# Attention steps dealt by a written table, and weights' splits issued ahead of them, in a fused attention, MoE and GLU kernel

## The chip, the core and the metric

The kernel runs on one core of one Trainium2 chip. The metric is the device time of one launch in microseconds (us): the median of three runs of the kernel before is 1403.98 us (1403.47 to 1404.71).

## What is computed

Three layers follow each other, all in float32. B = 2, H = 8 heads, S = 768, D = 64; N = B·S = 1536 tokens of width 512.

```python
# 1: attention, banded (96 local positions) plus 8 global keys, with a distance bias
scores = scale * q @ k.T + bias
a = softmax(where(is_global | is_local, scores, -1e9))
x = (a @ v) laid out as tokens x 512
# 2: MoE with 8 experts, gate P balanced by 8 Sinkhorn rounds
out = sum_e P[:, e:e+1] * (relu(x @ w1[e]) @ w2[e])        # w1[e]: 512 x 1024
# 3: gated linear unit
y = (sigmoid(out @ w_gate) * (out @ w_val)) @ w_out        # 512 x 1536 and back
```

## The kernel before

A product of float32 matrices is made of three TensorE passes over operands that are split into a high and a low part: `product` (lines 360 to 362) issues high·high, high·low and low·high. ScalarE (ACT) writes a high part by a copy that rounds, and GpSimd (POOL) or VectorE (DVE) subtracts it from the source for the low part: `split_one`, lines 203 and 204. The weights of an expert come in quarters; a quarter of `w1` and of `w2` lies in a buffer `raw` (two of them) and is split in halves, each half one ACT and one POOL instruction of 128x512.

The MoE is a row of **visits**, each one quarter of an expert for some tokens. A visit has two first products (12 passes of 128x384, ACT writes the relu `hh`, DVE the rest `hl`, lines 410 and 411), and after the first product of the next visit come its three second products (6 passes of 128x512). After each product `run_visit` calls `tick`. A tick does two things: `side`, a step of work that belongs elsewhere, and `ahead`, which splits the weights that come next (`ahead_steps`: the two halves of the next visit's `w1`, the two halves of this visit's `w2`, then `load`, two DMAs of 512 KB each that fill the `raw` buffer just freed). All DMAs of this stage are issued on SyncE's queue (SP), in program order.

In the first five visits (`NA` = 5) the side work is the second half of the attention: `banded_steps` yields a first part, then `None`, then 20 **attention steps** (`both`, here called s0 to s19). Each step issues the scores of two blocks of 128 queries (PE, line 981), their weights (DVE line 992, then two ACT exponentials each, line 998), the transposes of earlier weights (PE line 1023, copied out by ACT, line 1024: `aT`), the value products of still earlier ones (PE line 1037), and in half of the steps the transposes of the next q and k (PE line 924, copied out by ACT, line 930: `qT`, and by DVE: `kT`) with their loads. Transposes and products share a ring of four PSUM banks, so a product waits until the bank's last reader is done.

Ahead of the visits, two products of visit 0 are **begun** (`begun`: 9 of 12 passes); visit 0 ends them with 3 passes each. During the first part of the attention a pacer called `weights` splits the first weights. `Paced` deals a list of steps evenly over a number of ticks: with 20 steps over 18 ticks, each tick has one step, but the ninth and the last have two. The ticks are two in visit 0 (it has no second products ahead of it) and five in each later visit.

Of the kernel before, what the change touches and what calls it, by code (L numbers as in the profile page):

```python
# [33 lines left out]
class Ring:  # L34
    def __init__(self, items):
        self.items = list(items)
        self.n = 0
# [6 lines left out]
class Paced:  # L44
# [8 lines left out]
    def tick(self):  # L53
        self.n += 1
        upto = min(len(self.steps), len(self.steps) * self.n // self.ticks)
        while self.done < upto:
            self.steps[self.done]()
            self.done += 1

    def finish(self):  # L60
        while self.done < len(self.steps):
            self.steps[self.done]()
            self.done += 1


@with_exitstack
def tile_global_local_attention__then__sinkhorn_moe__then__glu(
# [100 lines left out]
    NA = NQ + 1  # L168
# [37 lines left out]
    def split_halves(r, h, lo, eng=nc.gpsimd):  # L206
        for half in range(2):
            cols = slice(half * 2 * FQ, (half + 1) * 2 * FQ)
            yield lambda cols=cols: split_one(r[:, cols], h[:, cols], lo[:, cols], eng)
# [5 lines left out]
    def second_steps(n):  # L215

        vis = visits[n]
        if vis["kind"] == "gate":
            return
        if vis["kind"] == "val":  # L220
            r = piece(vis["piece"] + 1)
        else:
            r = raw[vis["raw"]][:, 4 * FQ : 8 * FQ]
        eng = nc.vector if n == G0 + 1 else nc.gpsimd
        yield from split_halves(r, wh[vis["slot"]][1], wl[vis["slot"]][1], eng)

    def first_steps(n):

        vis = visits[n]
        if vis["load"]:  # L230
            r = raw[vis["raw"]][:, 0 : 4 * FQ]
            yield from split_halves(r, wh[vis["slot"]][0], wl[vis["slot"]][0])

    def ahead_steps(n):


        if 0 < n < F0 - 1:
            yield from first_steps(n + 1)
        if visits[n]["load"]:
            yield from second_steps(n)  # L240
            yield lambda b=visits[n]["raw"]: load(b)
# [16 lines left out]
    def sum_steps(n):  # L258

        a, (s1, s2, s3, s4) = w1_blocks(n), sums()  # L260
        for out, x, y, op in (
            (s1, a[1, 0], a[1, 1], ALU.add), (s2, s1, a[0, 0], ALU.subtract),
            (s4, a[0, 1], s2, ALU.subtract), (s3, a[0, 0], a[1, 0], ALU.subtract),
        ):
            yield lambda out=out, x=x, y=y, op=op: nc.gpsimd.tensor_tensor(
                out=out, in0=x, in1=y, op=op
            )

    def form_step(n, i):
        a, (s1, s2, s3, s4) = w1_blocks(n), sums()  # L270
        src = (a[0, 0], s1, s2, s4, s3, a[0, 1], a[1, 1])[i]
        h, lo = form(i)
        split_one(src, tall(h), tall(lo))
# [123 lines left out]
    def unit_first(n, c, tick):  # L397
        vis = visits[n]
        m = c[1] * P
        at = next_hid()  # L400
        hh, hl = hid[at]
        for f in range(2):
            w = wh[vis["slot"]][0], wl[vis["slot"]][0]
            if state["begun"]:
                ps = state["begun"].pop(0)
                first(w, c, f, ps, range(KD - 1, KD))
            else:
                ps = state["A"].next()[:, :m]
                first(w, c, f, ps)
            nc.scalar.activation(out=hh[:, f, :m], in_=ps, func=AF.Relu)  # L410
            nc.vector.scalar_tensor_tensor(
                out=hl[:, f, :m], in0=ps, scalar=0.0, in1=hh[:, f, :m].bitcast(F32),
                op0=ALU.max, op1=ALU.subtract,
            )
            tick()
        return [(n, c[0] + j, at, j) for j in range(c[1])]
# [30 lines left out]
    def flush(tick):  # L447
        pending, state["pending"] = state["pending"], []
        for unit in pending:
            unit_second(*unit)  # L450
            tick()

    def run_visit(n, tick, ahead, pace=None):


        chunks = visits[n]["chunks"]
        ahead = Paced(ahead, (chunks[0][1] + 2) * len(chunks) * (pace or PACE) // 12)
        side = tick

        def tick():  # L460
            side()
            ahead.tick()

        for c in chunks:
            pending = unit_first(n, c, tick)
            flush(tick)
            state["pending"] = pending
        ahead.finish()
# [237 lines left out]
    with tc.tile_pool(name="attn", bufs=1) as ap:  # L706
# [187 lines left out]
        def banded_tiles(fp):  # L894
            t = {}
            t["qT"] = [fp.tile([P, C], F32, name=f"qT{i}") for i in range(2)]
            t["kT"] = [fp.tile([P, UB, KW], F32, name=f"kT{i}") for i in range(2)]
            t["ks"] = [fp.tile([P, NG + NW], F32, name=f"ks{i}") for i in range(NP)]
            t["e"] = Ring(fp.tile([P, 2, KW], F32, name=f"e{i}") for i in range(LAG + 2))
            t["mn"] = Ring(fp.tile([P, 2], F32, name=f"mn{i}") for i in range(LAG + 2))  # L900
            sums = fp.tile([P, LAG + 2, 2, 2], F32, name="sums")
            nc.gpsimd.memset(sums, EPS)
            t["rs"] = Ring(sums[:, i] for i in range(LAG + 2))
            t["rr"] = Ring(fp.tile([P, 2], F32, name=f"rr{i}") for i in range(2))
            t["aT"] = Ring(fp.tile([P, 2, 2, P], F32, name=f"aT{i}") for i in range(2))
            return t
# [225 lines left out]
        with tc.If(banded > 0) as cmp:  # L1132
            with tc.tile_pool(name="banded", bufs=1) as fp:
                t = banded_tiles(fp)
                shared = Ring([bank[2], bank[3], bank[6]])
                state.update(S=bank[0:2], O=Ring(bank[4:6]), T=shared, X=shared)
                steps = list(banded_steps(t))
                begin = steps.index(None)
                weights = Paced([*[no_tick] * 5, *first_steps(0), no_tick], begin)

                def widen():
                    ring = state["T"]
                    at = ring.n % 3
                    ring = Ring([bank[7], *ring.items[at:], *ring.items[:at]])
                    state.update(T=ring, X=ring, A=ring, Y=ring)

                state["widen"] = widen
                for n, step in enumerate(steps[:begin]):
                    step()
                    weights.tick()  # L1150
                side = Paced(steps[begin + 1 :], 5 * NA - 7)
                early = list(first_steps(1))
                early.pop(0)()
                for n in range(NA):
                    run_visit(n, side.tick, [*early, *ahead_steps(n)])
                    early = []
                side.finish()
# [263 lines left out]
    side = Paced(gate_steps(), 5 * (NB0 - NA) + 5 * CB * NQ - 4)  # L1421
# [8 lines left out]
    for n in range(NA, F0):  # L1430
# [6 lines left out]
        if n < F0 - 1:  # L1437
# [3 lines left out]
        ahead = [  # L1441
            *ahead_steps(n), *sum_steps(F0), *(lambda i=i: form_step(F0, i) for i in range(4)),
            *second_steps(F0),
        ]
# [66 lines left out]
```

## Time and profile before

| | |
|---|---|
| Median of 3 runs | 1403.98 us |
| The profiled execution's own time | 1403.86 us |
| Its span, first to last instruction | 1402.1 us |
| TensorE busy | 1387.4 us, 99% |
| VectorE, ScalarE, GpSimd busy | 918.0, 564.8, 644.5 us |
| TensorE idle in 40 to 50 us, 50 to 60, 130 to 140 | 1.61, 0.70, 0.74 us |
| TensorE idle in 300 to 800 us | 0.0 us |

The profile is one execution. PE's matmuls are pipelined, so the distance between the starts of two of them says more than their durations. "PEld" is the loading of weights into the array. An idle time in brackets is that of the engine just before the row, with the instruction that ended it.

### The profile page before, as it was taken

How to read it: one execution, taken by the hardware profiler on the slowest of the kernel's cores; microseconds unless marked ns; L12 is line 12 of the kernel's file. 1: busy time of each engine (PE TensorE's matmuls, PEld its weight loads, DVE VectorE, ACT ScalarE, POOL GpSimd, SP SyncE). 2: the span in 40 equal slices, each digit the busy share in tenths (PEclk: the TensorE clock that was granted, in tenths of full speed). 3: DMA queues.
4: the chain of work that ended last, by engine and by line, in shares of the span. 5: the costliest groups of instructions: out<-in, count | busy, mean ns of one | idle time of the engine just before them, and what ended most of it. 6: DMA issues, size and time to landing. Idle time of an engine off the chain costs nothing. (4 is left out here: it accounts for less than half of the span.)

```text
span 1402.1 us, 20701 instructions
## 1 busy us (share of the span) xinstructions
PE 1387.4 (99%) x7425; PEld 1237.5 (88%) x7425; DVE 918.0 (65%) x1776; ACT 564.8 (40%) x1334; POOL 644.5 (46%) x757
## 2 busy tenths in 40 slices
PE   8999999999999999999999999999999999999998
PEld 5777799999999999999999999999999899999997
DVE  7676486776667667666776666667675665555446
ACT  6776323333333333333333333333333464444441
POOL 5664335534454453444545444454453464443440
PEclk9999999999999999999999999999999999999999
DMA  7860101212121222212212222121212011010002
GB/s 180 183 163 21 48 29 46 84 67 75 53 76 53 75 74 85 76 55 74 76 53 82 77 76 75 54 75 54 75 53 68 16 31 46 16 46 31 31 1 91
DMA packets 98944, 92.67 MB, mean 66 GB/s; under 512 B 55056, under 2 KB 73488, under 8 KB 98832
## 3 DMA queue, kind: packets, MB, share of 16 engines
q1 hardware_dynamic: 98544, 91.26, 21.3%
q8 instruction: 60, 0.98, 0.3%
q14 instruction: 52, 0.43, 0.1%
q10 hardware_dynamic: 288, 0.00, 0.0%
HBM read 78.66 MB, written 12.58 MB: 65 GB/s over the span
## 5 line engine op out<-in xcount | busy, mean ns | idle before, releaser
L435 DVE SCALAR_TENSOR_TENSOR acc<-bank,gate,acc 128x512 f32<-128x512 f32 x336 | 251.4, 748 | 229.1 <-PE bank L362 224.3
L204 POOL TENSOR_TENSOR wl<-raw,wh 128x256 fp32r<-128x256 f32 (+1 forms) x218 | 222.9, 1038 | 346.7 <-ACT wh L203 333.2
L360 PE MATMUL bank<-wh,hh 128*128 128x512 f32 x912 | 359.0, 394 | 0.4 <-DVE work L655 0.2
L362 PE MATMUL bank<-wh,hl 128*128 128x512 f32 x912 | 357.3, 392 | 0.0
L361 PE MATMUL bank<-wl,hh 128*128 128x512 f32 x912 | 355.9, 390 | 0.0
L360 PE MATMUL bank<-xh,wh 128*128 128x384 f32 x768 | 259.5, 338 | 1.7 <-DVE kept L551 0.9
L362 PE MATMUL bank<-xh,wl 128*128 128x384 f32 x768 | 257.6, 335 | 0.9 <-POOL wl L204 0.6
L361 PE MATMUL bank<-xl,wh 128*128 128x384 f32 x768 | 257.9, 336 | 0.0
L541 ACT ACTIVATE hh<-kept 128x384 fp32r<-128x384 f32 x168 | 88.2, 525 | 308.1 <-DVE kept L551 308.1
L362 PEld LDWEIGHTS bank<-wh,hl 128*128 128x128 f32 x912 | 171.1, 188 | 37.9
L204 POOL TENSOR_TENSOR wl<-work,wh 128x256 fp32r<-128x256 f32 x160 | 126.7, 796 | 148.3 <-ACT wh L203 147.9
L360 PEld LDWEIGHTS bank<-wh,hh 128*128 128x128 f32 x912 | 171.3, 188 | 24.2 <-DVE acc L435 0.8
L361 PEld LDWEIGHTS bank<-wl,hh 128*128 128x128 f32 x912 | 171.4, 188 | 22.7
L555 ACT ACTIVATE kept<-bank 128x384 f32<-128x384 f32 x240 | 117.4, 490 | 173.3 <-PE bank L362 171.9
L360 PE MATMUL bank<-th,wh 128*128 128x384 f32 x480 | 161.4, 336 | 0.0
L362 PE MATMUL bank<-th,wl 128*128 128x384 f32 x480 | 161.3, 336 | 0.0
L361 PE MATMUL bank<-tl,wh 128*128 128x384 f32 x480 | 161.0, 335 | 0.0
L551 DVE TENSOR_TENSOR kept<-bank,kept 128x384 f32<-128x384 f32 x240 | 132.2, 551 | 35.4 <-PE bank L362 34.8
L360 PEld LDWEIGHTS bank<-xh,wh 128*128 128x128 f32 x768 | 144.1, 188 | 12.6 <-ACT qT L930 1.5
L361 PEld LDWEIGHTS bank<-xl,wh 128*128 128x128 f32 x768 | 144.3, 188 | 9.3
L362 PEld LDWEIGHTS bank<-xh,wl 128*128 128x128 f32 x768 | 144.3, 188 | 1.0 <-POOL wl L204 1.0
L543 DVE SCALAR_TENSOR_TENSOR hl<-kept,hh 128x384 fp32r<-128x384 f32 x168 | 116.4, 693 | 1.4 <-ACT hh L541 1.4
(149 smaller groups left out, 1691.9 us busy)
## 6 DMA issues: line engine op xcount, KB each, us to landing
raw<-in_moe_w_dram SPq DMA_DIRECT2D x72, 512.0 KB, 4.3
glw<-work SPq DMA_DIRECT2D x36, 256.0 KB, 2.4
raw<-glw SPq DMA_DIRECT2D x18, 512.0 KB, 3.9
work<-in_moe_w_gate_dram SPq DMA_DIRECT2D x12, 512.0 KB, 3.9
work<-in_moe_w_val_dram SPq DMA_DIRECT2D x12, 512.0 KB, 4.3
work<-in_moe_w_out_dram SPq DMA_DIRECT2D x12, 512.0 KB, 3.8
qr<-in_q_dram SPq DMA_DIRECT2D x32, 96.0 KB, 3.0
kr<-in_k_dram SPq DMA_DIRECT2D x32, 96.0 KB, 2.8
```

Of the source, the lines that this page charges most:

```text
L204: eng.tensor_tensor(out=lo, in0=r, in1=h.bitcast(F32), op=ALU.subtract)
L360: nc.tensor.matmul(lhsT=ah, rhs=bh, start=first, stop=False, **mm)
L361: nc.tensor.matmul(lhsT=ah, rhs=bl, start=False, stop=False, **mm)
L362: nc.tensor.matmul(lhsT=al, rhs=bh, start=False, stop=end, **mm)
L435: nc.vector.scalar_tensor_tensor(out=a, in0=ps, scalar=gate[:, t, e : e + 1], in1=a, op0=ALU.mult, op1=ALU.add,)
L541: nc.scalar.activation(out=hh, in_=src, func=AF.Relu)
L543: lambda: nc.vector.scalar_tensor_tensor(out=hl, in0=src, scalar=0.0, in1=hh.bitcast(F32), op0=ALU.max, op1=ALU.subtract,)
L551: nc.vector.tensor_tensor(out=p, in0=ps, in1=kept, op=ALU.add)
L555: nc.scalar.activation(out=snap[:, i], in_=ps, func=AF.Copy)
```

## The change

Three edits, all in the attention stage: the 20 steps are dealt by a written list of counts (none at the first tick, which lies between the two begun products, two at the second tick of visits 2 and 3, one at each of the others up to the second tick of visit 4); in the first five visits a tick runs `ahead` before `side`; and the first weights' two splits are placed at 7/10 and 8/10 of the first part, not at 6/8 and 7/8.

```diff
+class Planned(Paced):
+
+    def __init__(self, steps, counts):
+        super().__init__(steps, len(counts))
+        self.counts = counts
+
+    def tick(self):
+        if self.n < len(self.counts):
+            for step in self.steps[self.done : self.done + self.counts[self.n]]:
+                step()
+            self.done += self.counts[self.n]
+        self.n += 1
...
         def tick():
-            side()
-            ahead.tick()
+            if n < NA:
+                ahead.tick()
+                side()
+            else:
+                side()
+                ahead.tick()
...
-                weights = Paced([*[no_tick] * 5, *first_steps(0), no_tick], begin)
+                weights = Paced([*[no_tick] * 6, *first_steps(0), *[no_tick] * 2], begin)
...
-                side = Paced(steps[begin + 1 :], 5 * NA - 7)
+                side = steps[begin + 1 :]
+                counts = [0, 1, *[1] * 5, *[1, 2, 1, 1, 1] * 2, 1, 1]
+                assert sum(counts) == len(side)
+                side = Planned(side, counts)
```

The first place is TensorE at the end of the two begun products (banks 70 and 65; `wh_80` and `wl_84` are visit 0's weights, `kT` and `qT` those of step s0). Before:

```order
L362 MATMUL bank_70<-xh,wl_84 128x384
L981 MATMUL bank_63<-kT_242,qT_240 128x256
L981 MATMUL bank_64<-kT_242,qT_240 128x256
L981 MATMUL bank_63<-kT_243,qT_241 128x256
L981 MATMUL bank_64<-kT_243,qT_241 128x256
L924 MATMUL bank_66<-ident,qr_120 128x128 x3
L924 MATMUL bank_69<-ident,kr_124 128x128 x3
L1023 MATMUL bank_70<-ident,e_250 128x128 x4
L360 MATMUL bank_65<-xh,wh_80 128x384
```

With the change:

```order
L376 MATMUL bank_70<-xh,wl_84 128x384
L374 MATMUL bank_65<-xh,wh_80 128x384
L375 MATMUL bank_65<-xl,wh_80 128x384
L376 MATMUL bank_65<-xh,wl_84 128x384
L999 MATMUL bank_63<-kT_242,qT_240 128x256
L999 MATMUL bank_64<-kT_242,qT_240 128x256
L999 MATMUL bank_63<-kT_243,qT_241 128x256
L999 MATMUL bank_64<-kT_243,qT_241 128x256
L942 MATMUL bank_66<-ident,qr_120 128x128 x3
L942 MATMUL bank_69<-ident,kr_124 128x128 x3
L1041 MATMUL bank_70<-ident,e_250 128x128 x4
L374 MATMUL bank_65<-xh,wh_82 128x384
```

The end of the second begun product now stands ahead of s0, and a whole product of visit 1 (`wh_82`) stands between s0 and s1.

The second place is ScalarE from the first product of visit 1 on. `wh_81` is visit 0's `w2`, `wh_83` visit 1's, and the `wh_80` here is visit 2's `w1`, split out of `raw_88` after that buffer's second load. Before:

```order
L203 ACTIVATE wh_81<-raw_88 128x512 x2
L410 ACTIVATE hh_78<-bank_69 128x384
L998 ACTIVATE e_251,sums<-e_251,mn_256 128x256 x2
L930 ACTIVATE qT_241<-bank_70,qs 128x384
L998 ACTIVATE e_252,sums<-e_252,mn_257 128x256 x2
L1050 ACTIVATE xh<-bank_67 128x384
L1024 ACTIVATE aT_263<-bank_66 128x512
L1024 ACTIVATE aT_262<-bank_69 128x512
L203 ACTIVATE wh_80<-raw_88 128x512
```

With the change:

```order
L217 ACTIVATE wh_81<-raw_88 128x512
L424 ACTIVATE hh_78<-bank_65 128x384
L217 ACTIVATE wh_80<-raw_88 128x512
L1016 ACTIVATE e_249,sums<-e_249,mn_254 128x256 x2
L1016 ACTIVATE e_250,sums<-e_250,mn_255 128x256 x2
L1042 ACTIVATE aT_263<-bank_66 128x512
L1042 ACTIVATE aT_262<-bank_69 128x512
L424 ACTIVATE hh_78<-bank_70 128x384
L217 ACTIVATE wh_80<-raw_88 128x512
L217 ACTIVATE wh_83<-raw_89 128x512
L1016 ACTIVATE e_251,sums<-e_251,mn_256 128x256 x2
L948 ACTIVATE qT_241<-bank_65,qs 128x384
```

Visit 2's first split of `w1` stood behind step s2 (exponentials of `e_251` and `e_252`); it now stands ahead of step s1 (`e_249` and `e_250`). On SP every row up to and past the load that fills `raw_88` for it stands as before.

The third place is GpSimd in the first part (`wl_84`: the low half of visit 0's first weights; `e`: POOL's share of the attention's normalisation). Before:

```order
L1011 TENSOR_SCALAR e_252<-e_252,rr_261 128x128
L1011 TENSOR_SCALAR e_248<-e_248,rr_260 128x256
L204 TENSOR_TENSOR wl_84<-raw_88,wh_80 128x512
L1011 TENSOR_SCALAR e_249<-e_249,rr_261 128x256
L204 TENSOR_TENSOR wl_84<-raw_88,wh_80 128x512
```

With the change:

```order
L1029 TENSOR_SCALAR e_252<-e_252,rr_261 128x128
L218 TENSOR_TENSOR wl_84<-raw_88,wh_80 128x512
L1029 TENSOR_SCALAR e_248<-e_248,rr_260 128x256
L218 TENSOR_TENSOR wl_84<-raw_88,wh_80 128x512
L1029 TENSOR_SCALAR e_249<-e_249,rr_261 128x256
```

Both subtractions moved up by one place, past the normalisations of `e_248` and `e_249`.

## Rows read from the trace of the kernel before

**Rows 1.** The page: TensorE's busy time, and its granted clock in 40 slices

```profile
PE 1387.4 (99%) x7425; PEld 1237.5 (88%) x7425; DVE 918.0 (65%) x1776; ACT 564.8 (40%) x1334; POOL 644.5 (46%) x757
...
PEclk9999999999999999999999999999999999999999
```

**Rows 2.** Busy times by stretch: stretch, sum, PE, PEld, DVE, ACT, POOL, PEclk, DMA, GB/s

```profile
300.00:800.00 500.00, 500.00 (x2516) 452.41 (x2515) 342.06 (x555) 178.06 (x396) 234.52 (x256) 1.00 0.21 71
```

**Rows 3.** Timeline, PE, 45 to 59 us: start us, us, engine line op out<-in xcount [idle before]

```profile
45.14 1.47 PE L981 MATMUL bank<-kT,qT 64*128 64x256 f32 x8 [0.56 <-DVE mn L992]
...
48.33 1.06 PE L1023 MATMUL bank<-ident,e 128*128 128x128 f32 x8 [0.92 <-DVE hl L411]
...
...
51.41 1.13 PE L981 MATMUL bank<-kT,qT 64*128 64x256 f32 x8
52.47 1.09 PE L1037 MATMUL bank<-aT,vo 128*64 128x128 f32 x16
...
55.95 0.45 PE L360 MATMUL bank<-xh,wh 128*128 128x384 f32 x1 [0.70 <-ACT qT L930]
...
58.23 1.14 PE L981 MATMUL bank<-kT,qT 64*128 64x256 f32 x8
```

**Rows 4.** Timeline, SP, 52 to 56 us: the issues around the second load of raw

```profile
52.45 0.96 SPq L724 DMA_DIRECT2D kr<-in_k_dram  x2
53.52 1.96 SPq L187 DMA_DIRECT2D raw<-in_moe_w_dram  x2
```

**Rows 5.** Line 187's DMA of 53.52 us, issue to landing; then all eight to 75 us

```profile
DMA to landing us min/median/max: 4.4/4.4/4.4
...
DMA to landing us min/median/max: 4.1/4.8/5.3
```

**Rows 6.** Timeline, ACT, 58 to 65 us

```profile
58.47 0.63 ACT L203 ACTIVATE wh<-raw 128x512 fp32r<-128x512 f32 x1
58.99 0.49 ACT L410 ACTIVATE hh<-bank 128x384 fp32r<-128x384 f32 x1
60.45 0.51 ACT L998 ACTIVATE e<-e,mn 128x256 f32<-128x256 f32 x1 [0.96 <-DVE mn L992]
...
61.45 0.56 ACT L930 ACTIVATE qT<-bank,qs 128x384 f32<-128x384 f32 x1
...
63.25 1.06 ACT L1024 ACTIVATE aT<-bank 128x512 f32<-128x512 f32 x2
64.21 0.62 ACT L203 ACTIVATE wh<-raw 128x512 fp32r<-128x512 f32 x1
```

**Rows 7.** Timeline, 134 to 136 us: the last attention step's copy and its value products

```profile
134.72 0.60 ACT L1024 ACTIVATE aT<-bank 128x512 f32<-128x512 f32 x1 [1.17 <-PE bank L1023]
135.37 0.42 PEld L1037 LDWEIGHTS bank<-aT,vo 128*64 128x64 f32 x8 [0.97 <-ACT aT L1024]
135.37 0.66 PE L1037 MATMUL bank<-aT,vo 128*64 128x128 f32 x8 [0.74 <-ACT aT L1024]
```

**Rows 8.** PEld at the start (512-column filler), then clock and busy times after the last matmul

```profile
1.58 0.15 PEld L763 LDWEIGHTS <-zeros 128*128 128x128 bf16 x1 [0.28 <-issue]
...
4.57 0.15 PEld L763 LDWEIGHTS <-zeros 128*128 128x128 bf16 x1 [0.28 <-issue]
4.99 0.31 PEld L763 LDWEIGHTS <-zeros 128*128 128x128 bf16 x2 [0.27 <-issue]
...
1401.00:1402.10 1.10, 0.00 (x0) 0.00 (x0) 0.00 (x0) 0.00 (x0) 0.00 (x0) 0.51 0.00 0
```

**Rows 9.** Timeline, PE, 87 to 90 us: the two steps of the ninth tick

```profile
87.77 1.26 PE L981 MATMUL bank<-kT,qT 64*128 64x256 f32 x8 [0.44 <-DVE mn L992]
...
89.54 1.21 PE L1037 MATMUL bank<-aT,vo 128*64 128x128 f32 x12 [0.51 <-ACT aT L1024]
```

**Rows 10.** Timeline, POOL, 33 to 38 us: a normalisation and the second low half

```profile
33.71 0.96 POOL L1011 TENSOR_SCALAR e<-e,rr 128x256 f32<-128x256 f32 x1
36.68 1.28 POOL L204 TENSOR_TENSOR wl<-raw,wh 128x512 fp32r<-128x512 f32 x1 [2.01 <-ACT wh L203]
```

## The prediction

> **What bounds the kernel now.** I read the page first: TensorE (PE) is busy 99% of the span, and its granted clock is full in every slice [rows 1]. So the kernel gets shorter only where PE stands still, and a new standstill counts in full: there is no slack behind it, since PE has no idle time at all from 300 to 800 us [rows 2]. Then I went through PE's timeline in the stretch that the change touches. There the waits are short: 0.56 us for VectorE ahead of the scores of step s1, 0.92 us ahead of its transposes, 0.70 us ahead of the second product of visit 1 [rows 3]; 0.44 and 0.51 us in the ninth tick, whose two steps have no product between them [rows 9]; 0.74 us at the end, where the last step follows the one before it directly [rows 7]. Together 3.87 us: this is about all that better dealing can win. Last I read SP and ACT, because the change moves ACT's splits, and a split waits for a DMA.
>
> **The split that moves ahead of its data.** Visit 2's first weights come from the second load of buffer raw 0. Its issue on SP starts at 53.52 us, right behind the issues before it (52.45 and 0.96 us) [rows 4], and lands 4.4 us later, at 57.92 [rows 5]. ACT takes it at 58.47 [rows 6]: only 0.55 us to spare. Nothing on SP ahead of this load is moved, and SP was not waiting but issuing, one DMA in about 0.5 us, so I take 57.92 for the changed kernel too.
>
> In the order of the changed ACT this split stands two attention steps and a product sooner: behind the relu of visit 1's first product, ahead of the exponentials of s1. That product had ended by 51.41 us before [rows 3], and now has one attention step less ahead of it, so ACT is there before 51 us and stands until 57.92. Behind it in ACT's queue are the four exponentials of s1 and the two copies `aT`; the value products of s2 wait for these on PE. PE reaches them early: before at 52.47 us, now with the second product of visit 1 also done (55.95 to 58.23, 2.28 us) and with the waits of 0.56 and 0.92 us gone, by some 53.3 us [rows 3].
>
> ACT from 57.92, each duration from the distance of starts [rows 6]: the split 0.52 (58.47 to 58.99), two pairs of exponentials 1.0 each (60.45 to 61.45), so the copies begin at 60.44. PE follows 0.65 us after such a copy begins (134.72 to 135.37) [rows 7]: it resumes at **61.1 us**, after standing for nearly 8. ACT goes on: the second copy ends at 60.44 + 0.96 = 61.40 (63.25 to 64.21 for two), the relu of visit 1's second product 0.5, two splits 1.04, a pair of exponentials 1.0, `qT` 0.56: 64.5. The next product, the first second product of visit 1, takes the PSUM bank that `qT` empties, so it starts at about 64.6. PE meanwhile needs 2.8 us for the rest of s2 (52.47 to 55.95, less the wait of 0.70), to 63.9, and waits once more.
>
> At this point the changed PE has done both begun products, s0 to s2 and both first products of visit 1. Before, the same set was done at 58.23 [rows 3]. The loss is 64.6 - 58.23 = **6.4 us**. The gains in between (2.18 us of waits) are inside it: because the end is pinned to a landing, coming sooner only lengthens the wait.
>
> **The clock after the wait.** Nothing in the trace before has PE idle for 8 us between matmuls. At the two ends of the run it shows this: after the last matmul the granted clock is still full for some 3 us and then falls (0.51 as the mean of the last 1.1 us), and when PE starts from rest, the filler of 512 columns loads its weights every 0.42 to 0.43 us from 1.58 to 4.99 us [rows 8], which is the lower level, 1.2 GHz, though the clock column says 1.00 there. I therefore take the clock to fall in the wait, and price the new start by these rows, 3.5 us at the lower level. From 61.1 these do half of 3.5 = 1.75 us of the 2.8, the rest goes at full speed: 65.7 in place of 64.6, **+1.1 us**, since part lies beside ACT's queue. Ends: 0 (the clock holds), 1.9 (half of 3.8, nothing covered). The Trainium skill, TensorE: Matmul & The Clock Gate, section on what matters for your kernels, says that an idle gap between bursts of matmuls puts PE back to half rate and asks to avoid such gaps: by that rule the sum stands, without it the time is 1.1 us lower; no run here has yet shown it inside a program.
>
> **The dealing.** The list puts two steps on the second tick of visit 3 where one stood, and takes the pair at the end apart. The nearest row for a pair without a product between is the ninth tick: 0.44 + 0.51 = **+0.95 us** [rows 9]; ends 0 and 1.9, as its exponentials are all full-width. The pair at the end had a wait of 0.74 us [rows 7], now covered by a whole product: **-0.74 us**; ends 0 and -0.97, PEld's figure.
>
> **The first splits.** They gain nothing in this sum, for whatever begins sooner ends in the wait of 57.92. By themselves they would be near zero as well: on POOL the second low half (1.28 us) now stands ahead of the normalisation of `e_249` (33.71 us) [rows 10], and waits for its ACT half; so PE would wait for that normalisation where it waited for the low half.
>
> **Sum.** 6.4 + 1.1 + 0.95 - 0.74 = 7.7 us on the profiled execution's 1403.86: **1411.6 us**; the median of the runs, 1403.98, lies 0.1 above that execution, which changes nothing here.
>
> **Rivals.** *The data is there in time* (not slower): if the load landed before ACT arrives, the change would do what its list says: -2.18 - 0.74 + 0.95 = -2.0, so 1401.9. The place is the second load of raw 0, the price one us for each us of landing, and it decides at about 57.92 - 7.7 = 50.2 us: an issue at some 45.8, about 15 issues of SP sooner. For it speaks that the split waited for nothing before, and that SP's time of issue comes from one execution; against it that SP issues without a gap and nothing of it is moved up. 5% for this, 3% for half of it. *The clock holds*: the same wait, 1410.5; for it, that no row shows a fall between matmuls. 25%. *More is late behind the wait*: the loads of q for step s8 wait for PE to read that buffer in s2, so SP stands too, and with it the loads of v and the next raw, each some 8 us later; against it, these had ten us and more to spare. One more wait of 3 us gives 1414.6. 10%. The forecast keeps 57%.
>
> **How the numbers follow.** Landing times of this load's kind lie between 4.1 and 5.3 us [rows 5], so -0.3 to +0.9; with the clock at 0 and the second pair at 0 the forecast's own range begins at 1409.2, and with all high ends it reaches 1415. I give 1407.5 to 1414.5: it takes in the clock's rival, most of the later waits and some of a shorter wait, and leaves out the first rival. A measurement of this kernel tells about 0.2% (2.8 us) from no change: faster 0.04, same 0.05, slower 0.91.
>
> **What would show it.** Right: ACT idle some 8 us ahead of a split (line 217) until a raw DMA, near 49 to 58 us; PE's value products (line 1055) waiting for `aT` to about 61; the rows of 0.56, 0.92 and 0.70 us gone; a granted clock under 1 after the wait; a pair of waits in the second tick of visit 3. Wrong: that split without a wait, or a landing well before 55 us; then the reading of SP as bound by its issues has failed.

## The result, and the profile after

The changed kernel takes 1411.48 us (median of 5 runs, 1410.96 to 1412.37) against 1403.98 before: ratio 1.0054, interval [1.0043, 1.0066]. The forecast was 1411.6, in a range from 1407.5 to 1414.5. The profiled execution took 1411.96 us with a span of 1410.1, where the span before was 1402.1: 8.0 us more in the spans, 7.5 in the medians. Times below are medians without one execution, of the kernel with four issues sooner, that took 1522.8 us at a granted clock of 0.851.

The page of the changed kernel, TensorE's (PE's) busy time and granted clock, answers to [rows 1]; one slice is no longer full:

```profile
PE 1389.7 (99%) x7425; PEld 1240.1 (88%) x7425; DVE 917.4 (65%) x1776; ACT 564.8 (40%) x1334; POOL 644.2 (46%) x757
...
PEclk9899999999999999999999999999999999999999
```

PE's timeline where the two begun products end, which answers to [rows 3]:

```profile
52.10 1.14 PE L999 MATMUL bank<-kT,qT 64*128 64x256 f32 x8
61.21 1.97 PE L1055 MATMUL bank<-aT,vo 128*64 128x128 f32 x16 [7.98 <-ACT aT L1042]
...
66.02 0.75 PE L374 MATMUL bank<-wh,hh 128*128 128x512 f32 x1
```

The waits of 0.56, 0.92 and 0.70 us are gone, and in their place PE stands for 7.98 us, for the copies `aT` of step s1. ACT's timeline says why (it answers to [rows 6], and line 217 is the split):

```profile
48.26 0.61 ACT L217 ACTIVATE wh<-raw 128x512 fp32r<-128x512 f32 x1
48.78 0.47 ACT L424 ACTIVATE hh<-bank 128x384 fp32r<-128x384 f32 x1
58.09 0.63 ACT L217 ACTIVATE wh<-raw 128x512 fp32r<-128x512 f32 x1 [8.84 <-DMA raw<-in_moe_w_dram]
58.62 0.49 ACT L1016 ACTIVATE e<-e,mn 128x256 f32<-128x256 f32 x1
...
60.59 1.05 ACT L1042 ACTIVATE aT<-bank 128x512 f32<-128x512 f32 x2
```

ACT is done with the relu of visit 1's first product at 49.25 and stands 8.84 us in front of the split of visit 2's weights; the exponentials of s1 and the copies behind it come after. The transfer it waits for was issued by SP at its old place in the order, 0.49 us sooner than in the profile before, and took 5.0 us (the first of the two; the rows are from SP's timeline and from line 201's instructions of 52 to 56 us; compare [rows 4, 5]):

```profile
53.03 2.28 SPq L201 DMA_DIRECT2D raw<-in_moe_w_dram  x2
```

```profile
DMA to landing us min/median/max: 4.4/4.7/5.0
```

The busy times by stretch (columns as in [rows 2]) show the clock, the third figure from the right: 1.00 up to 53 us, 0.50 (the level of 1.2 GHz) for all that PE does from 61.2 to 66, and 1.00 again from 68:

```profile
50.00:53.00 3.00, 3.00 (x21) 2.54 (x20) 1.80 (x11) 0.00 (x0) 0.23 (x1) 1.00 0.77 176
53.00:61.20 8.20, 0.24 (x4) 0.00 (x0) 0.78 (x3) 3.11 (x11) 2.41 (x3) 0.71 0.50 158
61.20:66.00 4.80, 4.79 (x30) 4.46 (x31) 3.23 (x14) 3.81 (x10) 4.04 (x4) 0.50 0.14 32
66.00:68.00 2.00, 2.00 (x10) 1.42 (x10) 1.27 (x5) 2.00 (x8) 1.73 (x5) 0.85 0.71 157
```

Behind this stretch only short waits are left, of the kind of [rows 7, 9] (PE's timeline, the rows with a wait from 90 to 140 us, and one at 145.53). They are the two-step ticks of visits 2 (0.78, and 0.24 a little later) and 3 (0.51), and a step near the end (0.40):

```profile
93.96 1.16 PE L1055 MATMUL bank<-aT,vo 128*64 128x128 f32 x16 [0.78 <-ACT aT L1042]
101.61 0.50 PE L374 MATMUL bank<-wh,hh 128*128 128x512 f32 x1 [0.24 <-ACT qT L948]
124.03 1.15 PE L1055 MATMUL bank<-aT,vo 128*64 128x128 f32 x16 [0.51 <-ACT aT L1042]
137.65 1.15 PE L1055 MATMUL bank<-aT,vo 128*64 128x128 f32 x16 [0.40 <-ACT aT L1042]
...
145.53 0.66 PE L1055 MATMUL bank<-aT,vo 128*64 128x128 f32 x8
```

The last row is the last step's value products, which waited 0.74 us before [rows 7] and wait no more. The 0.40 us belong to an earlier step, which had such a wait before as well:

```profile
128.77 1.14 PE L1037 MATMUL bank<-aT,vo 128*64 128x128 f32 x16 [0.41 <-ACT aT L1024]
```

The set of work that the prediction counted (both begun products, s0 to s2, visit 1's first products) was done at 58.23 before and is done at 66.02 now: 7.79 of the 8.0 us are lost here.

### The profile page after: what moved, and what is told of

The parts are those of the page before. It is cut to its first block, busy times and chain, and to the rows that moved or that the text cites. A ratio compares the mean times of both kernels' runs of the same rounds, so it can differ in the third digit from the quotient of the medians.

```text
span 1410.1 us, 20699 instructions
## 1 busy us (share of the span) xinstructions
PE 1389.7 (99%) x7425; PEld 1240.1 (88%) x7425; DVE 917.4 (65%) x1776; ACT 564.8 (40%) x1334; POOL 644.2 (46%) x757
```

## The experiments

The theory is that one transfer that lands at 58 us sets the end of this stretch, through ACT's queue, and that the clock adds to it. The rivals are that the dealt steps or the order within a tick cost this by themselves, and that the clock costs nothing. Each kernel below was traced in one execution. Most kernels below issue that transfer sooner. They share one function (lines shift by 10 to 16 for it):

```diff
+    def load_sooner(eng=None):
+        state["sooner"] = 0, state["load", 0]
+        src = queues[0][state["load", 0]][0]
+        (eng or nc.sync).dma_start(out=raw[0][:, 0 : 4 * FQ] ..., in_=src ...)
...
         for j, src in enumerate(queues[b][at]):
+            if j == 0 and (b, at) == state["sooner"]:
+                continue
```

### Four issues sooner

```diff
-weights = Paced([*[no_tick] * 6, *first_steps(0), *[no_tick] * 2], begin)
+weights = Paced([*[no_tick] * 6, *first_steps(0), load_sooner, no_tick], begin)
```

> The changed kernel, but the first half (w1) of the second load of raw 0 is issued four SP issues sooner, ahead of q and k of one unit. Theory (the split waits for the landing, and the end is pinned to it): four issues at 0.5 us are 2.1 us, so the split on ACT begins at 55.9 to 56.0 in place of 58.09, the wait of PE for aT is 5.9 us in place of 7.98, and the time is 1409.4 (2.1 below the changed kernel's 1411.5). Rival (the wait comes from the dealt steps, not from the load): the wait of 8 us stays, 1411.5. Rival (SP is held by something else than its issues): the load is issued at 53 us all the same, 1411.5.

Measured: 1411.12 us, ratio 1.005 [1.0037, 1.0063]; by the median hardly less than the changed kernel. SP's, ACT's and PE's timelines:

```profile
52.41 0.41 SPq L213 DMA_DIRECT2D raw<-in_moe_w_dram  x1
...
57.06 0.63 ACT L227 ACTIVATE wh<-raw 128x512 fp32r<-128x512 f32 x1 [7.82 <-DMA raw<-in_moe_w_dram]
...
60.19 1.97 PE L1065 MATMUL bank<-aT,vo 128*64 128x128 f32 x16 [6.96 <-ACT aT L1052]
```

The number was missed, and the link held: the load went out only 0.62 us sooner, since SP was later in this execution from early on (the first load of raw 1 at 30.92 us, in the changed kernel at 29.90). From issue to split it took 0.41 us less, so the split began 1.03 us sooner, and PE's wait is 1.02 us shorter. By the time alone its rivals (1411.5) are not told from it. A place in SP's queue is not a time.

### Twelve and twenty issues sooner

As above, and the loads of q, k and v of one unit (of two, kept in a list, in the second kernel) are held until the load of w1 is issued; shown for twelve:

```diff
 def loads():
+    if u == 5:                      # twenty: u in (4, 5)
+        state["held"] = loads_now
+    else:
+        loads_now()
...
-load_sooner, no_tick], begin)
+lambda: (load_sooner(), state["held"]()), no_tick], begin)
```

> As the kernel before it in this list, but the load of w1 also goes ahead of q, k and v of one more unit: twelve issues in all, 6.3 us sooner. Theory: issue at 46.7 us, landing at 51.1 to 51.7; ACT is there at 49.3, so PE's wait for aT shrinks from 7.98 us to between 1.0 and 1.6, and the clock has no time to fall. 6.7 us of wait and about 1.75 us of lower clock go: 1403.0, between 1402.4 and 1403.8. Rival (the wait is of the dealing, or two-step ticks are dear): over 1408. Rival (the q, k and v put back are late in their turn): a new wait for a DMA on PE, over 1405.

> The changed kernel, the first half of the second load of raw 0 ahead of q, k and v of two more units on SP: 20 issues sooner (as in the run with twelve, four for the one unit and eight for each of the other two). Theory: issue at about 42.6 us, landing by 47.3, ahead of ACT, which comes for it at 49.3: ACT's split has no wait, PE waits at most 0.2 us for aT and nothing more for the bank of qT; the set is done at 56.0 in place of 57.96 with twelve: 1.3 + 0.6 us less than that run's 1403.6, 1401.7, between 1401.0 and 1402.4; this is the changed deal with its data there. Rival (a second bound stands close behind): 1403.2 or more.

Measured: 1403.61 us with twelve, ratio 1.0 [0.9992, 1.0009]; 1402.35 with twenty, 0.9992 [0.9983, 1.0001]. ACT's and PE's timelines, first with twelve, then with twenty:

```profile
51.45 0.63 ACT L227 ACTIVATE wh<-raw 128x512 fp32r<-128x512 f32 x1 [2.13 <-DMA raw<-in_moe_w_dram]
...
54.58 1.14 PE L1071 MATMUL bank<-aT,vo 128*64 128x128 f32 x16 [1.26 <-ACT aT L1058]
57.96 0.50 PE L384 MATMUL bank<-wh,hh 128*128 128x512 f32 x1 [0.57 <-ACT qT L958]
```

```profile
49.17 0.62 ACT L227 ACTIVATE wh<-raw 128x512 fp32r<-128x512 f32 x1
...
53.66 1.14 PE L1071 MATMUL bank<-aT,vo 128*64 128x128 f32 x16
57.05 0.50 PE L384 MATMUL bank<-wh,hh 128*128 128x512 f32 x1 [0.57 <-ACT qT L958]
```

This settles the main question. With the transfer there in time the same deal, the same order and the same first splits take 9.1 us less (1411.48 to 1402.35; 8.7 if each is set against the runs of the kernel before that were made beside it), ACT's split has no wait, PE has none for `aT`. A wait of 0.57 us for the bank that `qT` empties stays, which the expectation of 1401.7 had at nothing; the time lies within its range.

### The load from POOL's queue

```diff
-load_sooner, no_tick], begin)
+lambda: load_sooner(nc.gpsimd), no_tick], begin)
```

> The changed kernel, the first half of the second load of raw 0 issued by POOL at about 38 us, where POOL has 2.8 us of idle time, and not by SP. The issue on ACT waited for landings of SP's DMAs (7.6 us); the program gives a DMA of POOL a semaphore of its own, so no such wait is expected. Theory: the load lands by 45 at the latest, ACT's split does not wait: 1401.7, as with 20 issues sooner; if POOL's issue takes longer than its idle time, its low half of visit 0 comes later and PE waits up to 1 us more at 43 us: 1402.7. Rival: a wait of POOL in place of ACT's, as before: 1408 or more.

Measured: 1402.47 us, 0.9991 [0.9982, 1.0]. POOL's timeline:

```profile
38.11 0.95 POOL L213 DMA_DIRECT2D raw<-in_moe_w_dram  x1
41.01 1.29 POOL L228 TENSOR_TENSOR wl<-raw,wh 128x512 fp32r<-128x512 f32 x1 [1.95 <-ACT wh L227]
```

The issue takes 0.95 us of POOL, inside its idle time, and nothing of q, k or v is moved: the same gain by another way. The Trainium skill, DMA: Bandwidth & Descriptors, section Issuing engines are not separate DMA queues, says that issuing on several engines saves only the time of issuing, usually small beside the DMA itself. The trace agrees for one DMA: SP's issue of this load took 0.41 us with four issues sooner, and its landing 4.6. What the trace adds is the queue: the issues ahead of this load on SP, most at some 0.5 us, held it to 53 us, where it could go at 38.

### The load from ACT's queue

```diff
-load_sooner, no_tick], begin)
+lambda: load_sooner(nc.scalar), no_tick], begin)
```

> The changed kernel, but the first half (w1) of the second load of raw 0 is issued by ACT, right behind its copy xh at about 36 us, instead of by SP at 53. Theory (all of the loss is the landing): issue at 36 to 38, landing by 43, ACT's split of visit 2's weights runs without a wait at 49.3, PE waits at most 0.2 us for aT and about nothing for the bank that qT empties; the first second product of visit 1 starts at 56.0, where it was 57.96 with twelve issues sooner and 66.0 in the changed kernel: 1401.7, between 1401.0 and 1402.5. An issue on ACT took 0.42 to 0.45 us at the program's start; if that lies on the path, 0.45 more. Rival (there is a second bound near, such as the bank of qT): 1403.5, as with twelve issues sooner.

Measured: 1411.34 us, 1.0054 [1.004, 1.0067]. ACT's and PE's timelines, and a stretch of the busy times:

```profile
43.52 0.40 ACTq L213 DMA_DIRECT2D raw<-in_moe_w_dram  x1
43.97 1.08 ACT L1052 ACTIVATE aT<-bank 128x512 f32<-128x512 f32 x2 [7.62 <-DMA vo<-in_v_dram]
...
44.62 2.04 PE L1065 MATMUL bank<-aT,vo 128*64 128x128 f32 x16 [4.21 <-ACT aT L1052]
...
46.00:48.00 2.00, 2.00 (x11) 1.67 (x8) 0.56 (x1) 1.01 (x2) 0.21 (x1) 0.50 1.10 312
```

A miss of 9.6 us, though visit 2's split indeed had no wait. But ACT stood 7.6 us ahead of the issue itself, until a transfer of v that SP had issued landed. In the built program, the issue on ACT waits for a semaphore (`DMAHW5_49`) that it shares with SP's DMAs, the one on POOL does not:

```
L213 DMA raw_88<-in_moe_w_dram 128x4x256 [waits DMAHW5_49,Pool_49]   (issued by ACT)
L213 DMA raw_88<-in_moe_w_dram 128x4x256 [waits Pool_49]             (issued by POOL)
```

So the same kind of wait, 14 us sooner, cost as much: an in-order queue that holds the softmax, and something in it that waits for a transfer. PE's own standstill is only 4.21 us here. The first second product of visit 1 starts at 65.54, where it starts at 57.03 with the load on POOL's queue; the rest of these 8.5 us goes with the clock, which was at 0.50 for work ahead of the stop (38 to 40 us) and behind it (44 to 50 us).

Two variants of this kernel have the same wait. In the first, the load's own place in ACT's queue moves too, from the ninth of ten steps to the last of eight.

> The kernel before it in this list, with the first splits back at their later place. Theory (the sooner first splits only exchange one wait for another): PE waits for a low half again (0.6 us at about 38) and no longer 0.7 for the normalisation of an e: within 0.3 us of the kernel before it in this list. Rival (they are worth their wait): 0.6 to 1.0 us slower than it.

> The same load on ACT's queue, with the order within a tick undone (attention step ahead of the split). With the data there in time, theory: the splits no longer delay anything, so this order is the question of 0.52 us of ACT per tick: the waits for the bank of DVE's hl and of qT (0.92 and 0.70 us in the kernel before) come back in part, 0.5 to 1.5 us slower than the same with the changed order, some 1402.5. Rival (the changed order is worth nothing in itself): the same within 0.3 us.

Measured: 1407.72 us (1.0026 [1.0016, 1.0035]) and 1412.73 (1.0061 [1.0047, 1.0075]). Both missed: the first is 3.6 us below the kernel that it should have equalled, the second 10.2 above its figure. They say little of their questions, since ACT's wait was 7.48 and 7.95 us in them, with PE's standstill after it 5.09 and 6.12. The last section of experiments asks both again, with the data in time.

### PE kept busy through the wait

```diff
 # in both(w), ahead of the value products
+if w == begin + 4:
+    ring = state["X"]
+    free = ring.items[ring.n % len(ring.items)]
+    for _ in range(34):
+        nc.tensor.matmul(out=free, lhsT=zeros[:, 0:P], rhs=zeros, start=True, stop=True)
```

> The changed kernel with 34 matmuls of zeros (512 columns) into a free PSUM bank ahead of the value products that wait, so that PE works through most of the wait; they add nothing to the output. Theory (the clock falls in the wait and costs beyond it): 34 of about 0.21 us are 7.2 of the 7.98 us, so PE resumes at 61.2 as before but at full clock; the rest of that step takes 2.8 us in place of 4.8, the bank that qT empties is then the end (64.5), and nothing is slow behind it: about 1.75 us less, 1409.7, granted clock 1.00 throughout. Rival (the clock costs nothing on the path): 1411.5. If the lower clock costs only what ACT does not hide: 1410.4.

Measured: 1411.16 us, 1.0051 [1.0038, 1.0064]; a miss by the time. ACT's and PE's timelines, and the stretch after the wait:

```profile
59.09 0.63 ACT L217 ACTIVATE wh<-raw 128x512 fp32r<-128x512 f32 x1 [9.77 <-DMA raw<-in_moe_w_dram]
...
53.24 7.51 PE L1129 MATMUL bank<-zeros 128*128 128x512 bf16 x34
62.22 1.14 PE L1055 MATMUL bank<-aT,vo 128*64 128x128 f32 x16 [1.47 <-ACT aT L1042]
65.60 0.50 PE L374 MATMUL bank<-wh,hh 128*128 128x512 f32 x1 [0.56 <-ACT qT L948]
...
60.70:66.00 5.30, 3.27 (x33) 2.70 (x33) 3.67 (x15) 4.95 (x16) 4.55 (x5) 1.00 0.15 34
```

The clock holds at 1.00, but the transfer landed 1.0 us later than in the changed kernel (59.09 for 58.09), and the two nearly cancel. Counted from the start of the split, the first second product comes after 6.51 us in place of 7.93, and the end of the span after 1350.1 (1409.2 - 59.09) in place of 1352.0 (1410.1 - 58.09). So the clock costs 1.4 us up to that product and 1.9 in all, at one landing. With twelve issues sooner, where the clock held too, these are 6.51 and 1350.15: the same. The time of this run by itself does not decide, since the rival's 1411.5 lies inside its interval; the rows do. And the price is not fixed: with four issues sooner the clock was back sooner (0.86 as the mean of 64 to 66 us), the two counts are 7.72 (64.78 - 57.06) and 1351.2 (1408.3 - 57.06), and the low clock cost 1.2 and 1.1 us.

### The order within a tick alone, and undone

```diff
 # undone, in the changed kernel; the other kernel has it alone, in the kernel before
-            if n < NA:
-                ahead.tick()
-                side()
-            else:
-                side()
-                ahead.tick()
+            side()
+            ahead.tick()
```

> The changed kernel with the order within a tick undone (attention step ahead of the weights' split), the counts and the sooner first splits kept. Theory: the split that waits for the landing at 57.9 us now stands behind the exponentials and copies aT of step s1, ahead of those of s2 with qT. PE no longer waits for aT but, some 2.8 us later, at the first second product for the bank that qT empties: ACT from 57.9, a split 0.5, relu 0.5, two exponentials 1.0, qT 0.6, so 60.6; PE waits 4 to 5 us there, and the set is done at 60.7 in place of 58.23 before and 66.0 in the changed kernel. With 0.3 us for the dealing 1406.7, and up to 1.9 more if the clock falls in this wait: 1406.7 to 1408.6. Rival (the order alone is the cause): 1402 to 1403. Rival (the order has no part in it): 1411.5.

> The kernel before with one edit, the split ahead of the attention step in a tick; the steps are dealt as before, and the load is where it was. Theory: the split stands ahead of the exponentials of s2 and of qT, behind which the scores of s3 wait. ACT from the landing at 57.9: split 0.5, exponentials 1.0, qT 0.6, so those scores begin at 60.1 in place of 58.8: 1.3 us slower, 1405.2; with SP's issue one us later, as in two of the runs above, 1406.3. Rival (the order alone makes the loss): 1409 or more. Rival (it wins the short waits): 1402.

Measured: 1410.66 us undone (1.0048 [1.0035, 1.0061]), 1409.48 alone (1.0039 [1.0025, 1.0052]). PE's timelines, and one stretch, first of undone and then of alone:

```profile
60.77 1.09 PE L1037 MATMUL bank<-ident,e 128*128 128x128 f32 x4 [5.13 <-DVE hl L425]
62.61 0.79 PE L374 MATMUL bank<-wh,hh 128*128 128x512 f32 x1 [0.75 <-ACT qT L944]
...
64.00:66.00 2.00, 2.00 (x6) 1.17 (x6) 0.99 (x2) 2.00 (x5) 0.72 (x2) 0.50 0.51 103
```

```profile
58.45 0.69 PE L360 MATMUL bank<-xh,wh 128*128 128x384 f32 x1 [4.07 <-ACT qT L934]
...
60.00:62.00 2.00, 2.00 (x8) 2.00 (x7) 0.35 (x1) 0.72 (x2) 0.80 (x1) 0.50 0.60 132
```

Both expectations were too low, and both times fall on a rival's figure: alone it is in "1409 or more", and undone its interval takes in 1411.5. So PE's rows have to decide here, and they show the loss as a wait behind the same split in both. Undone, I had named the right cause and the wrong first waiter: the relu behind the split feeds DVE's `hl`, whose bank the transposes of `e` need a little ahead of the bank of `qT`; and the split began at 59.02, 0.9 us later than in the changed kernel. Alone, the waiter is not s3's scores but the second first product of visit 1, for the bank of `qT`, as in [rows 3] but for 4.07 us in place of 0.70. The clock is at 0.50 after waits of 5 and 4 us; alone, I had left it out, and undone, allowed up to 1.9 us for it. What follows: the order alone loses 5.5 us, the counts with the first splits 6.8, each against the runs beside it; together they lose 7.5 and not the sum, since each puts the split ahead of its data and the end is pinned to the landing. The landings differ in these executions (the split began at 56.32, 59.02 and 58.09), so the three losses can be compared only roughly: from the split to the end of the span they took 1350.1, 1349.9 and 1352.0 us.

### The two small parts, with the data in time

Both edits are those shown, made on the kernel with twenty issues sooner. With the first splits late, the load moves by one place as well; SP issued it at 42.61 in place of 43.66 us, and the split of visit 2's weights has no wait in either.

> The kernel with 20 issues sooner (1402.35), the first splits of visit 0 back at their later place. Theory (these splits only exchange one wait for another): the waits of 0.5 us for the bank of qT and 0.8 us for the normalisation of an e on POOL go, the wait of 0.6 us for the second low half at about 38 us comes back: within 0.3 us of 1402.35, rather below it by the 0.3 to 0.6 us by which the two waits are longer than the one. Rival (they are worth their wait): 1403 or more.

> The kernel with 20 issues sooner (1402.35), the order within a tick undone: attention step ahead of the split. Theory (with the data there, this order is worth the short waits for the bank of DVE's hl and of qT, 0.92 and 0.70 us in the kernel before): 0.5 to 1.5 us slower, 1402.9 to 1403.9. Rival (the order is worth nothing, the counts made the gain): within 0.3 us of 1402.35.

Measured: 1401.85 us with the first splits late (0.9987 [0.9978, 0.9996]), 1403.28 with the order undone (0.9997 [0.9988, 1.0006]). PE's timeline, waits up to the first second product: the changed first splits (which also have the 0.57 us shown above), then the late ones:

```profile
34.86 0.63 PE L1057 MATMUL bank<-ident,e 128*128 128x128 f32 x4 [0.52 <-ACT qT L958]
36.63 0.66 PE L1057 MATMUL bank<-ident,e 128*128 128x128 f32 x4 [0.78 <-POOL e L1045]
```

```profile
37.59 0.44 PE L386 MATMUL bank<-xh,wl 128*128 128x384 f32 x1 [0.64 <-DMA vo<-in_v_dram]
56.23 0.51 PE L384 MATMUL bank<-wh,hh 128*128 128x512 f32 x1 [0.56 <-ACT qT L958]
```

The sooner first splits exchange one wait of 0.64 us for two of 0.52 and 0.78. (The view puts the 0.64 down to a DMA; the row reads the low half `wl`, which POOL had only just written, and before the change the view names POOL there.) The new one, 0.52 for the copy `qT`, comes since ACT now has a split ahead of that copy. They cost 0.5 us by the medians and 0.8 by the first second product (57.05 against 56.23); the intervals of the two kernels overlap, so it is the rows that show it. The order within a tick is worth 0.9 us by the medians (1403.28 against 1402.35) and 0.7 by the spans (1401.4 against 1400.7): inside what was expected, and at the edge of what these runs can tell. The kernel with twenty issues sooner and the first splits left late is the fastest of all: 1401.85, below both kernels of this case, 0.13% under the one before.

## Why the prediction was right

**The landing.** Predicted 57.92, from an issue at 53.52 and 4.4 us; the issue was at 53.03, the landing took 5.0, the split began at 58.09. That nothing ahead of this load on SP would change its order held. That the two agree within 0.2 us is luck: the issue came 0.49 us sooner and the landing took 0.6 longer, and in three other kernels with the same order on SP the split began at 56.32, 59.02 and 59.09. What the prediction had right is that the end of the stretch hangs on the landing, wherever it falls.

**PE's wait.** Predicted from some 53.3 to 61.1; measured 53.23 to 61.21. ACT's sum behind the split (0.52, two pairs of 1.0, PE 0.65 after the copies begin) came out within 0.1 us. At full clock the set would have been done at 58.09 + 6.51 = 64.60, where the prediction had 64.6 before its term for the clock.

**The clock.** Predicted +1.1 us with ends of 0 and 1.9: the set was forecast for 65.7 and done at 66.02. The size is nearer the upper end: 1.4 us up to that product and 1.9 in all, by the run with PE kept busy (1.2 and 1.1 where the clock was back sooner). I had taken 3.5 us at the lower level from the start of the program; here PE was at 0.50 from 61.2 to past 66 (0.70 as the mean of 66 to 67), more than five. The Trainium skill, TensorE: Matmul & The Clock Gate, section Why this matters for your kernels, says that a long enough idle gap between bursts of matmuls puts PE back to half rate. The trace agrees, with 0.50 in the row of 61.2 to 66. So the rival by which the clock holds (1410.5, 25%) is out, by that row and not by the time, whose interval takes in 1410.5.

**The dealing.** Predicted +0.95 for the second two-step tick and -0.74 for the end, +0.21 together. The waits in PE's rows of the attention behind the set are 0.44, 0.51, 0.41 and 0.74 before and 0.78, 0.24, 0.51 and 0.40 after: 2.10 and 1.93, so -0.17. The end gave 0.74 back, as forecast; the two pairs together cost 0.58 more than the one before (0.78 + 0.24 + 0.51 - 0.95), where I had put 0.95. The spans agree: 8.0 - 7.79 = 0.2 us remain behind the set, of which 0.5 (1.9 - 1.4) is clock, so -0.3. The sum came out because this miss and that of the clock have opposite signs. The prediction's list of short waits (3.87 us) also leaves out the 0.41.

**The first splits.** Predicted near zero by themselves; they cost 0.5 to 0.8 us. The step that failed is that PE would wait for the normalisation *in place of* the low half at equal price: that wait is 0.78 for 0.64, and the wait of 0.52 for `qT`, behind the split on ACT, was not in the account at all. In the changed kernel (0.68 and 0.74) this is hidden, as predicted, by the landing.

**The first rival.** Data in time was priced at 1401.9, 2.0 us below the profiled execution before; the runs with the data in time are at 1402.35 and 1402.47, some 1.1 to 1.2 below the kernel before in their comparison. Most of the difference is the first splits: without them it is 2.0 (1401.85 against 1403.86). That this equals the forecast is not shown term by term: the 0.57 us for the bank of `qT` stay in all these kernels, and the price of 2.0 had no such wait. The point from which it decides, a landing at 50.2 us, fits: with ACT's split at 51.45 PE still waited 1.26 us, at 49.17 not at all.

**More late behind the wait.** It did not come: behind 66 us no wait for a DMA stands in PE's rows. SP did stand, as that rival had it, its next load of q going out at 64.05 us where it went at 55.57 before; the loads had that much to spare.

## What to carry to other kernels

Before a step is moved forward in an in-order queue, look up when its data lands, not only when its engine is free: in the kernel before, this split had 0.55 us to spare, and no view of waits shows a wait that was just missed. Where the gain is sought in waits of under 1 us, one instruction that waits for a DMA ahead of the softmax undoes all of them, and the clock added 1 to 2 us to a standstill of 7 to 8. Move the load first, then the step that reads it; an idle queue (POOL's, here) can carry the load past a backlog.

## What the runs showed that was not expected

**SP's issue times are not fixed by their order.** The same load stood at the same place in five kernels and was issued at 53.52 (before), 53.03 (changed), 54.83 (PE kept busy), 54.46 (order undone) and 52.09 us (order alone). With the order undone, SP's timeline has a single issue of 1.98 us among ones of 0.5:

```profile
49.22 0.48 SPq L756 DMA_DIRECT2D vo<-in_v_dram  x1
49.75 1.98 SPq L738 DMA_DIRECT2D vo<-in_v_dram  x1
51.78 0.49 SPq L756 DMA_DIRECT2D vo<-in_v_dram  x1
```

In the same 2.5 us the trace has one transfer on queue q8, of the kind "instruction"; with PE kept busy it is an issue of 1.70 us at 50.40, again beside such a transfer; in the changed kernel that transfer falls at 53 to 54.8, into the second half of this load. That loading instructions holds SP is suggested by this and was not tested. SP also waits a little: from 25 to 52 us its waits before the change are 1.2 us for a landing of `raw` and 1.9 us in all for PE, so "not waiting but issuing" in the prediction is nearly right, and not quite.

**A DMA issued by another engine can wait for the first engine's transfers**: 7.6 us on ACT, through a shared semaphore, against none on POOL.

**The clock fell after shorter stops, too**: it was at 0.50 when PE resumed after waits of 4.07 us (order alone) and 5.13 us (order undone), and stayed there to about 64 and 67 us. After the wait of 1.26 us with twelve issues sooner it stayed at 1.00 (busy times of 48 to 60 us). In one execution, that with the load on ACT's queue, it fell without any long stop, between 36 and 40 us, behind waits of 0.69 and 0.74 us; six other kernels show these waits there to within 0.01 us, and 1.00. What made the difference is open.
